# Attention in steps of three key blocks instead of two, with six tiles of exponentials and two of totals

## Chip, cores, metric

One core of one Trainium2 chip. The metric is device time in microseconds (us), the lower the better. Every run told of here is of state fast.

## The reference, cut to what matters

Hash attention on 4 batches of 8 heads, 768 tokens of 64 dimensions, then a feed-forward layer with a squared relu on 3072 tokens. All in float32; the two weight matrices come as float64 and the kernel rounds them itself.

```python
q_bits = (einsum('bhsd,dk->bhsk', q, proj) > 0);  k_bits = ...      # 6 bits a token
mask   = q_bucket[:, :, :, None] == k_bucket[:, :, None, :]
scores = where(mask, scale * q @ k.T, -1e9)
attn   = exp(scores - max); attn = attn / (sum(attn) + 1e-9)
x      = (attn @ v).transpose(0, 2, 1, 3).reshape(3072, 512)
out    = square(maximum(x @ w_in, 0)) @ w_out
```

## The kernel before

Sixteen pairs of heads go through attention one after the other. For each of the six key blocks of a pair, `score` makes scores in PSUM on PE (tile `st`; hash bits first, then features) and exponentials from them on ACT (tile `e`, one of a ring of four); `add_up` sums exponentials on DVE; `attend` multiplies them by the values on PE (tile `xo`). `finish` belongs to the pair before: hash of the next pair, totals, the last two value blocks, and the spread of the reciprocals (L445). Beside this, each pair rounds two pieces (a and b) of the float64 weights: load into `raw` on the SyncE queue, `part_weight` (L141, L145) on DVE, `place_power` (L158, L159) on ACT, `round_weight` (L169 to L177) on DVE, and a store. In six pairs DVE also makes sums for the feed-forward part. All queues run in the order written here:

```python
for pr in range(NP):                       # 16 pairs of heads
    a, b = 2 * pr, 2 * pr + 1
    ...
    if pr + 2 < NP:
        load_pair(pr + 2)                  # 8 loads of q and k, SyncE queue
    ...
    features(pr + 1, ...)                  # DVE, wanted by the next hash
    round_weight(b - 2); load_weight(b)    # load_weight: raw piece, SyncE queue
    score(pr, 0); score(pr, 1)
    finish(pr - 1, prepare)                # hash, totals, attend(pr-1, 4..5), spread
    add_up(pr, 1)
    weigh(pr + 1); normalize(pr - 1)
    part_weight(a)
    score(pr, 2); score(pr, 3)
    place_power(a)
    attend(pr, 0); attend(pr, 1)
    add_up(pr, 2); add_up(pr, 3)
    load_values(pr + 1)
    round_weight(a)
    part_weight(b)                         # here in the kernel before
    load_weight(a + 2)
    score(pr, 4); score(pr, 5)
    place_power(b)
    attend(pr, 2); attend(pr, 3)
    add_up(pr, 4)
    if pr in sums: ...                     # pairs 4, 5, 8, 9 (sums_in), 10, 11 (sums_x)
```

(Conditions for the first and last pair are cut.)

## Time and profile before

| | kernel before |
|---|---|
| median, at the time of the prediction | 908.31 us (3 runs, 908.2 to 908.92) |
| span of the profiled run, mean granted clock | 906.5 us, 0.998 |
| attention, to the first feed-forward matmul | 347 us, PE busy throughout from 35 us on |
| one pair, from spread to spread | 20.55 us |

The last line is read from the starts of the L445 matmuls (the spread, one a pair). "Pair n takes" means below: from the spread of pair n-1 to the spread of pair n, a stretch that holds all of DVE's sums of pair n. The lines of the profile that matter are in the prediction; idle time and DMA are read there as the page gives them.

### The profile page before, as it was taken

The page shows a single profiled execution, that of the slowest core. Times are in us where ns is not written, and L with a number is a line of the kernel's source. Part 1 is how long each engine was busy: PE and PEld are TensorE (multiplying, and loading weights), DVE is VectorE, ACT ScalarE, POOL GpSimd, SP SyncE. Part 2 cuts the span into 40 slices and gives each one's busy share as a digit, 9 for nine tenths or more (in the row PEclk, how much of TensorE's full clock was granted, in tenths as well). Part 3 has the DMA queues.
Part 4 walks back from the last instruction along what each step waited for, and adds up shares of the span by engine and source line. Part 5 has one row for each costly group of instructions (what it writes and reads, how often), then busy time and mean ns, then how long its engine had stood idle before and what let it go on. Part 6 is the DMA issues. An engine that isn't in the chain of part 4 may idle for free.

```text
span 906.5 us, 11859 instructions
## 1 busy us (share of the span) xinstructions
PE 882.5 (97%) x4358; PEld 504.4 (56%) x4358; DVE 697.4 (77%) x1010; ACT 364.2 (40%) x593; POOL 91.7 (10%) x149
## 2 busy tenths in 40 slices
PE   6999999999999999999999999999999999999996
PEld 3344444444444444444588864445888644458885
DVE  3788899889998885887768766667887766678775
ACT  4888787788878752222111112222111122221110
POOL 2000000000000000562100021111000211110002
PEclk9999999999999999999999999999999999999999
DMA  9467978789977425997974745546856554445566
GB/s 183 86 124 137 231 171 186 141 276 241 230 181 153 128 91 172 278 282 214 319 227 147 187 81 150 150 138 190 298 162 173 96 148 137 135 142 158 153 167 112
DMA packets 253343, 158.14 MB, mean 174 GB/s; under 512 B 166432, under 2 KB 215584, under 8 KB 253280
## 3 DMA queue, kind: packets, MB, share of 16 engines
q1 hardware_dynamic: 219984, 84.43, 40.6%
q10 hardware_dynamic: 22560, 37.50, 14.1%
q0 software_dynamic: 10736, 35.40, 13.0%
q8 instruction: 36, 0.59, 0.3%
q14 instruction: 27, 0.22, 0.1%
HBM read 119.28 MB, written 38.01 MB: 174 GB/s over the span
## 4 chain that ended last, share of the span: by engine, by line
PE 90%; DMA 4%; DVE 2%; ACT 1%; issue 1%; POOL 0%; ACTq 0%; SPq 0%; DVEq 0%
PE acc L657 54%; PE st L375 18%; PE xo L402 14%; DMA w_unit<-w_in 3%; PE tot L420 3%; PE hash L327 1%; ACT bits L337 1%; DMA out_dram<-ot 1%; DVE peaks L698 0%; DMA q_nat<-in_q_dram 0%; PE tp L300 0%; POOL out_dram L818 0%; DVE b L747 0%; ACTq L787 0%; DVE ot L811 0%
## 5 line engine op out<-in xcount | busy, mean ns | idle before, releaser
L379 ACT ACTIVATE e<-st 128x1024 f32<-128x1024 f32 x192 | 145.4, 810 | 68.8 <-PE st L375 63.9
L657 PE MATMUL acc<-x,w_unit 128*128 128x512 f32 x384 | 169.6, 593 | 0.6 <-DMA w_unit<-w_in 0.6
L375 PE MATMUL st<-feat,feat 64*128 64x512 f32 (+1 forms) x768 | 152.4, 488 | 0.0
L657 PE MATMUL acc<-b,leaf 128*128 128x256 f32 x600 | 133.3, 379 | 2.3 <-DMA leaf<-w_out 2.3
L402 PE MATMUL xo<-e,v_nat 128*64 128x512 f32 (+1 forms) x768 | 134.8, 492 | 0.0
L657 PE MATMUL acc<-t_x,w_unit 128*128 128x512 f32 x288 | 127.8, 593 | 0.2 <-ACT one L664 0.2
L657 PEld LDWEIGHTS acc<-b,leaf 128*128 128x128 f32 x600 | 113.8, 190 | 19.8 <-DMA leaf<-w_out 3.5
L657 PEld LDWEIGHTS acc<-x,w_unit 128*128 128x128 f32 x384 | 72.8, 190 | 91.5 <-issue 89.2
L402 PEld LDWEIGHTS xo<-e,v_nat 128*64 128x64 f32 x768 | 51.4, 136 | 82.4 <-issue 70.9
L657 PEld LDWEIGHTS acc<-t_x,w_unit 128*128 128x128 f32 x288 | 54.5, 190 | 70.0 <-issue 67.7
L375 PEld LDWEIGHTS st<-feat,feat 64*128 64x128 f32 x768 | 67.0, 190 | 35.5 <-issue 27.6
L392 DVE TENSOR_TENSOR total<-total,e 128x1536 f32<-128x1536 f32 x48 | 84.2, 1755 | 1.7
L746 DVE TENSOR_TENSOR h<-acc,two 128x512 f32<-128x512 f32 x24 | 16.6, 691 | 84.9 <-PE acc L657 84.9
L657 PE MATMUL acc<-t,leaf 128*128 128x256 f32 x336 | 76.8, 380 | 0.6 <-DVE t L481 0.3
L664 ACT COPY two<-acc 128x512 f32<-128x512 f32 (+1 forms) x45 | 21.9, 487 | 131.7 <-PE acc L657 128.6
L337 ACT ACTIVATE bits<-hash,lifts 32x384 bf16<-32x384 f32 x124 | 71.1, 573 | 6.5 <-PE hash L327 3.2
L664 ACT COPY one<-acc 128x512 f32<-128x512 f32 (+1 forms) x45 | 21.9, 487 | 118.8 <-PE acc L657 77.7
L657 PEld LDWEIGHTS acc<-t,leaf 128*128 128x128 f32 x336 | 63.5, 190 | 10.6 <-DVE t L481 1.1
L375 PE MATMUL st<-bits,bits 64*128 64x256 bf16 (+1 forms) x384 | 63.9, 328 | 3.4 <-ACT bits L337 2.2
L747 DVE SCALAR_TENSOR_TENSOR b<-h 128x512 f32<-128x512 f32 x96 | 64.3, 690 | 2.5
L657 PE MATMUL acc<-b_t,leaf 128*128 128x256 f32 x240 | 54.2, 380 | 1.3 <-issue 1.3
L657 PEld LDWEIGHTS acc<-b_t,leaf 128*128 128x128 f32 x240 | 45.4, 190 | 8.1 <-issue 2.1
(122 smaller groups left out, 866.4 us busy)
## 6 DMA issues: line engine op xcount, KB each, us to landing
leaf<-w_out ACTq DMA_DIRECT2D x142, 256.0 KB, 3.0
w_unit<-w_in SPq DMA_DIRECT2D x24, 896.0 KB, 5.7
raw<-in_moe_w_in_dram SPq DMA_DIRECT2D x16, 512.0 KB, 5.5
raw<-in_moe_w_out_dram SPq DMA_DIRECT2D x16, 512.0 KB, 4.5
w_out<-sums POOLq DMA_DIRECT2D x16, 448.0 KB, 8.0
v_nat<-in_v_dram SPq DMA_DIRECT2D x16, 384.0 KB, 4.7
x_all<-x_t SPq DMA_DIRECT2D x16, 384.0 KB, 3.1
x<-x_all POOLq DMA_DIRECT2D x3, 2048.0 KB, 12.5
```

What stands on the lines that cost most here:

```text
L327: nc.tensor.matmul(out=banks[g * NR_B:(g + 1) * NR_B, h, 0:HS], lhsT=projs[rows], rhs=feat[pr, w][rows, c * HS:(c + 1) * HS], start=True, ...
L337: nc.scalar.activation(out=t[h * D:h * D + NR_B, c * HS:(c + 1) * HS], in_=hashed[pr, w][at, h, 0:HS], func=ACTF.Sign, scale=HUGE, bias=li ...
L375: nc.tensor.matmul(out=st[:, h, 0:hi - lo], lhsT=src[pr, 1][rows, key], rhs=src[pr, 0][rows, lo:hi], start=first, stop=not first,)
L379: nc.scalar.activation(out=e[:, :, lo:hi], in_=st[:, :, 0:hi - lo], func=ACTF.Exp, scale=scale)
L392: nc.vector.tensor_tensor(out=totals[pr], in0=in0, in1=weights[pr, kt][:, :, 0:S], op=ALU.add)
L402: nc.tensor.matmul(out=xo[h * D:(h + 1) * D, lo:hi], lhsT=nat[pr, "v_nat"][:, h, kt * D:(kt + 1) * D], rhs=weights[pr, kt][:, h, lo:hi], s ...
L420: nc.tensor.matmul(out=tot[g * 32:(g + 1) * 32, 0:HS], lhsT=ones, rhs=src[:, h, c * HS:(c + 1) * HS], start=src is totals[pr], stop=src is ...
L657: nc.tensor.matmul(out=acc[to], lhsT=a(i), rhs=b(i), start=first and i == 0, stop=last and i == n - 1, skip_group_check=True,)
L664: nc.scalar.copy(out=t, in_=acc[of])
L746: nc.vector.tensor_tensor(out=h, in0=one, in1=two, op=ALU.add)
L747: nc.vector.scalar_tensor_tensor(out=out[:, r], in0=h, scalar=0.0, in1=h, op0=ALU.max, op1=ALU.mult)
```

## The change

Fewer, longer runs of score and value blocks: three by three instead of two by two. That needs the exponentials of a whole pair to stand, so six tiles instead of four, and a second tile of totals, as the next pair's first adds now come before the last pair's totals are used. To make room, `x_t` and the input sums fall from two buffers to one. On the way, the splitting and powers of piece b move up beside those of piece a.

```diff
-    p_x = first.enter_context(tc.tile_pool(name="p_x", bufs=2))
+    p_x = first.enter_context(tc.tile_pool(name="p_x", bufs=1))
-    NRING = 4
+    NRING = SB
-            totals[pr] = p_n.tile([P, 2, S], FP32, name="total")
+            totals[pr] = p_n.tile([P, 2, S], FP32, name="total", bufs=2)
-        sums = [p_t.tile([P, nf, NS], FP32, name=f"s_in{n}", bufs=2) for n in range(4)]
+        sums = [p_t.tile([P, nf, NS], FP32, name=f"s_in{n}") for n in range(4)]
-        for kt in (SB - 2, SB - 1):            # in finish
+        for kt in range(SB // 2, SB):
             attend(pr, kt)
 ...
-            score(pr, 0)
-            score(pr, 1)
+            for kt in range(3):
+                score(pr, kt)
+            for kt in (1, 2):
+                add_up(pr, kt)
             if pr > 0:
                 finish(pr - 1, prepare if more else None)
-            add_up(pr, 1)
 ...
             part_weight(a)
-            score(pr, 2)
-            score(pr, 3)
+            part_weight(b)
+            for kt in range(3, SB):
+                score(pr, kt)
             place_power(a)
-            attend(pr, 0)
-            attend(pr, 1)
-            for kt in (2, 3):
+            place_power(b)
+            for kt in range(3):
+                attend(pr, kt)
+            for kt in (3, 4):
                 add_up(pr, kt)
 ...
             round_weight(a)
-            part_weight(b)
             if more:
                 load_weight(a + 2)
-            score(pr, 4)
-            score(pr, 5)
-            place_power(b)
-            attend(pr, 2)
-            attend(pr, 3)
-            add_up(pr, 4)
```

## The prediction

> **What bounds the kernel now.** I first read the first part of the page, then the busy time by stretches, because an average over two stages hides each stage. The stretches are my choice: the first pair of heads (4.80 to 35.17), the other pairs (35.17 to 346.98) and the feed-forward part.
>
> ```profile
> PE 882.5 (97%) x4358; PEld 504.4 (56%) x4358; DVE 697.4 (77%) x1010; ACT 364.2 (40%) x593; POOL 91.7 (10%) x149
> ...
> 4.80:35.17 30.37, 25.17 (x149) 11.84 (x150) 16.43 (x23) 19.52 (x30) 2.21 (x11) 1.00 1.10 177
> 35.17:346.98 311.81, 311.81 (x2363) 142.46 (x2361) 269.25 (x366) 239.33 (x352) 0.79 (x1) 1.00 0.71 167
> ```
>
> The columns of a stretch are its length, then busy us of PE, weight loads, DVE, ACT, POOL, the clock and the DMA. From 35.17 on PE is busy for all 311.81 us, with DVE at 86% and ACT at 77%. So no wait is there to remove: only less time on PE itself can shorten this stage. The first pair is the exception: 5.2 us of its 30.37 are idle on PE.
>
> Next the chain that ended last, over one pair. It is nothing but PE:
>
> ```profile
> 123.02 2.74 PE xo L402 x16
> 125.76 0.08 PE xo L445 x4
> 125.84 3.34 PE st L375 x24
> 129.18 2.74 PE xo L402 x16
> 131.92 3.34 PE st L375 x24
> 135.26 2.74 PE xo L402 x16
> 138.00 3.34 PE st L375 x24
> 141.34 0.81 PE hash L327 x16
> 142.15 1.43 PE tot L420 x16
> ```
>
> A pair takes 143.58 - 123.02 = 20.56 us: three runs of two score blocks (st), three of two value blocks (xo), one hash, one total and one spread of reciprocals (L445). Last I read PE's timeline where st hands over to xo, taking starts, as ends of matmuls are modelled:
>
> ```profile
> 126.97 0.60 PE L375 MATMUL st<-feat,feat 64*128 64x256 f32 x4
> 127.40 0.38 PE L375 MATMUL st<-bits,bits 64*128 64x512 bf16 x2
> ...
> 128.59 0.60 PE L375 MATMUL st<-feat,feat 64*128 64x256 f32 x4
> 129.11 2.81 PE L402 MATMUL xo<-e,v_nat 128*64 128x512 f32 x16
> ```
>
> The same four matmuls are followed after 0.43 us by another st, but after 0.52 us by an xo. Note the forms: st has weights of 64*128 (two row tiles), xo of 128*64 (two column tiles). The hand-over costs time although nothing is waited for.
>
> **What the Trainium skill says.** (1) "TensorEngine Tiling (Array Packing)", Key Properties: a change of tiling mode, not merely of tile, drains the TensorE. The trace agrees: about 0.1 us more at the change from 64*128 to 128*64. (2) "TensorE: Matmul & The Clock Gate", Part 2, step 5 (NX overlap): in a stream the drain of one matmul overlaps the fill of the next; a drain is what a mode change loses. The page has no cost for the change, so I take it from the trace. (3) "Perfetto Trace Analysis", Tensor Engine Instruction: the end of a matmul is an estimate; here consecutive records overlap (0.60 long at 126.97, the next at 127.40), hence starts only. (4) The TensorE page's section on the array (engine queue depths): ScalarE and VectorE are strict FIFO. So program order on DVE and ACT decides what a late operand holds up; the trace shows DVE idle before L426 with later adds queued behind it.
>
> **The change, part by part.**
>
> *Fewer mode changes.* Before, a pair alternates st,st | xo,xo three times; after, st x3 | xo x3 twice. All matmuls stay. From single starts in the trace: one st block to the next inside a run is 1.617 us, so a run of two (3.34) holds 3.34 - 3.234 = 0.106 us of change; one xo block to the next is 1.291 us, so a run of two (2.74) holds 2.74 - 2.582 = 0.158 us. One round trip costs 0.264 us. Each pair loses one: runs become 3 x 1.617 + 0.106 = 4.96 and 3 x 1.291 + 0.158 = 4.03, and the pair 20.56 - 0.26 = 20.29. For pairs 1 to 15: 15 x 0.264 = 4.0 us off, all on the path.
>
> *The first pair.* In PE's timeline of the kernel before:
>
> ```profile
> 22.84 1.62 PE L327 MATMUL hash<-feat,projs 64*32 64x384 f32 x16 [0.60 <-ACT e L379]
> ...
> 29.32 0.39 PE L375 MATMUL st<-bits,bits 64*128 64x512 bf16 x2 [0.39 <-ACT bits L337]
> ...
> 31.78 0.29 PE L375 MATMUL st<-bits,bits 64*128 64x256 bf16 x2 [1.21 <-ACT e L379]
> ```
>
> PE loses 0.6 + 0.4 + 1.2, and about 0.75 in a hash twice its later 0.81 (its features came late from DVE). The steady run starts at 35.17 with six st, a hash and four xo done. After: st(0) to st(5) go through from 13.26, to 22.24 + 2 x 1.617 = 25.5; hash to 26.4; three xo to 30.4. ACT ends the exponentials 1.1 us after st, at 26.6; eight signs of 0.586 to 31.3; the powers of two weight pieces now come together, 2 x 1.37, to 34.0; only then the first exponential of pair 1. PE takes up pair 1 at 31.3 and, with three score buffers, stalls when the third is full (34.0) until the first exponential ends (35.0). At 31.3 it has done what the old one has at 35.17 less one xo (1.3): ahead by 2.6; less the stall of 1.0: 1.6 us gained.
>
> *DVE.* Its work stays; its order does not. Flip (the reciprocals) now queues behind two adds (1.75 each) of the next pair instead of ahead of one, and normalize follows it nearer. I set out a pair from the end of the spread, S, with start-to-start times from the timeline: normalize 0.1 to 2.1; splitting two pieces 2 x 0.67, to 3.4; adds of blocks 3 and 4, 3.53, to 6.9; rounding piece a waits for its power (ACT ends three exponentials at 6.0, then 1.4: 7.5), 1.93, to 9.4; features of the next pair 1.76, to 11.2; rounding piece b 1.97, to 13.2; adds of blocks 1 and 2 wait for exponentials to 15.1, to 16.9; flip to both 1.26, to 18.2. PE wants it at 4.96 + 4.03 + 4.96 + 0.81 + 1.43 + 4.03 less the last 0.1 of those: about 20.1. Slack 1.9. But six pairs (4, 5, 8, 9, 10, 11) also compute sums, 2.53 by DVE's timeline. Then features end at 13.7 (hash starts at 13.9: just in time), the adds end at 19.2, and both at 20.5: 0.4 late. What shows how tight these are already:
>
> ```profile
> 102.54 0.58 DVE L426 STREAM_TRANSPOSE flip<-tot 128x384 f32<-128x384 f32 x1 [3.21 <-PE tot L420]
> ...
> 123.09 0.58 DVE L426 STREAM_TRANSPOSE flip<-tot 128x384 f32<-128x384 f32 x1 [0.68 <-PE tot L420]
> ```
>
> DVE's only idle time in a pair is 3.2 us, in one with sums 0.7. New waits: 6 x 0.4 = 2.2 us (rounded down, as the last one or two run lighter operations). They don't pile up: the wait for the power absorbs a late normalize.
>
> *Buffers.* Six rings let a pair's exponentials stand until the next pair; two totals let add 1 start ahead of the old total's use. x_t and the input sums fall to one buffer. x_t is written once in 20 us and its DMA lands in 3.1; the sums likewise in 2.9. xo has one buffer: normalize ends at S + 2.1, the next xo at S + 4.96. Nothing here is on the path. At the seam, DVE's first result of the feed-forward part overlies x_t; it may wait 0.6 us for the DMA, and DVE then has 5.3 us idle in the trace before, so PE does not see it.
>
> *Feed-forward.* Untouched; it starts earlier and ends as much earlier.
>
> Sum: -4.0 - 1.6 + 2.2 = -3.4 us, so 908.3 - 3.4 = 904.9.
>
> **Rivals.** (a) *DVE takes the bound in more pairs.* For: 86% busy, and both waits of the new order (for exponential 2, for the spread) sit in one FIFO. Against: 1.9 us of slack in ten pairs. If 0.4 were lost in all fifteen, 6 us would eat the gain: about 908.7. (b) *No DVE wait at all,* if adds run a little closer than I laid them: 908.3 - 5.6 = 902.7. (c) *The start gives nothing:* ACT's two power pieces ahead of pair 1's exponentials stall PE longer than 1.0; the same six and fifteen then give 908.3 - 1.8 = 906.5. (d) *Hidden transfers.* The changed loading order could make a weight piece late. Against: in the list of PE's waits attention shows no DMA after the first transposes, and raw pieces land in 5.0 us with over 10 to spare. No change of time.
>
> **Range and chances.** The switch term is counted and repeated fifteen times; I trust it to 0.5 us. The start may be off by 1.5, the DVE term by 2. That gives 902.8 to 906.9. Two per cent is 18 us, more than three times anything worked out: within 2% 0.98, each side 0.01.
>
> **What would show it.** Chain: st runs of 36 in 4.96 and xo runs of 24 in 4.03, pairs of 20.29 us. PE's waits: an L445 wait on DVE of some 0.4 us in six pairs and none in others; a stall of about 1 us on ACT e near 34. DVE's waits: the idle time before flip goes, and appears before recs (L455), about 2 us in pairs without sums. If xo after xo across the longer run still costs 2.74 per two, the switch account is wrong; if L445 or hash wait in ordinary pairs, (a) holds; if pairs run at 20.29 throughout, (b).

## The result, and the profile after

911.12 us median (910.82 to 913.05, 6 runs) against 908.95 (908.2 to 910.44, 6 runs) for the kernel before: ratio 1.0027, 95% interval 1.0014 to 1.004. The prediction said 904.9, in a range of 902.8 to 906.9. It is wrong, in sign too: slower by about 2 us instead of faster by 3.4. (The two are within 2% of each other, to which it gave 0.98. Ratios here and below are the mean time of one kernel's fast runs over that of the other's of the same rounds, so not quite the ratio of the medians quoted.)

The part that the change was made for came out as worked out. The chain of the kernel after, over one pair (start, us, what):

```profile
63.39 4.96 PE st L375 x36
68.35 4.03 PE xo L402 x24
72.38 4.96 PE st L375 x36
77.34 0.81 PE hash L327 x16
78.15 1.43 PE tot L420 x16
79.57 4.03 PE xo L402 x24
```

Runs of 36 score matmuls in 4.96 us and of 24 value matmuls in 4.03, as predicted to the last digit. The pair takes 20.29.

But not every pair does. From the starts of L445 in the two traces, spread to spread:

| pair | 1 to 3 | 4 | 5 | 6 | 7 | 8 | 9 | 10 | 11 | 12 | 13 | 14 | 15 |
|---|---|---|---|---|---|---|---|---|---|---|---|---|---|
| before | 20.55 | 20.55 | 20.55 | 20.55 | 20.55 | 20.55 | 20.55 | 20.55 | 20.55 | 20.55 | 20.55 | 19.75 | 16.40 |
| after | 20.29 | 20.64 | 20.69 | 20.34 | 20.29 | 20.64 | 26.06 | 21.08 | 20.87 | 20.34 | 20.29 | 19.49 | 14.53 |

(The sums are in pairs 4, 5 and 8 to 11. The last two are shorter as the hash and then the next pair's scores fall away.) Over 20.29, pairs 4 to 12 lose 8.3 us; pair 9 alone 5.8. The account closes: first spread 0.66 us earlier, fourteen pairs 0.26 shorter (3.6), the last one 1.87 shorter, 8.3 lost: 2.1 us later at the first feed-forward matmul, which is where the traces put it (342.09 and 344.24 us after the first matmul of each).

What pair 9 loses it for is in DVE's timeline of the kernel after (start, us, what; in brackets the idle time before, and what ended it):

```profile
208.64 0.42 DVE L141 TENSOR_SCALAR power<-raw 128x512 uint32<-128x512 uint32 x1
208.97 0.42 DVE L145 TENSOR_SCALAR top<-raw 128x512 uint32<-128x512 uint32 x1
214.06 0.43 DVE L141 TENSOR_SCALAR power<-raw 128x512 uint32<-128x512 uint32 x1 [4.67 <-DMA raw<-in_moe_w_out_dram]
```

Piece a is split; piece b isn't there yet, and DVE stands for 4.67 us with the adds, the rounding and the features of the next pair queued behind. Piece b was late because of the SyncE queue, in the kernel after:

```profile
198.88 6.60 SPq L278 DMA_DIRECT2D q_nat<-in_q_dram  x4
205.52 2.23 SPq L278 DMA_DIRECT2D k_nat<-in_k_dram  x4
207.85 1.74 SPq L188 DMA_DIRECT2D w_out<-out_piece  x1
209.64 0.43 SPq L128 DMA_DIRECT2D raw<-in_moe_w_out_dram  x1
```

Issuing eight loads of q and k holds the queue for 8.8 us (ahead of them stood the four stores of pair 8's sums, 2.52 us, much as in the kernel before, 2.73), the store of the piece just rounded follows, and only then is raw issued, 3.3 us after the spread of pair 8 at 206.33; it lands 4.4 us later. ("Perfetto Trace Analysis", DMA Instruction: HWDGE, in the Trainium skill: the time shown for a DMA on this queue is the sequencer's, for lock, descriptors and semaphore, and only at its end is it free for the next instruction. This trace agrees.) The kernel before issued it at the same place in the pair (3.3 us after the spread, at 207.80), but asked for it later:

```profile
211.12 0.43 SPq L128 DMA_DIRECT2D raw<-in_moe_w_out_dram  x1
```

```profile
216.58 0.42 DVE L141 TENSOR_SCALAR power<-raw 128x512 uint32<-128x512 uint32 x1
```

The first line is from its SyncE queue, the second from its DVE: 5.5 us from issue to use, about 1 us more than a landing of 4.4. The old order was safe by one microsecond, and the change took away 5.7 (from 8.8 to some 3.1 us after the spread).

What DVE's stop did to PE, in PE's timeline of the kernel after:

```profile
219.98 0.60 PE L375 MATMUL st<-feat,feat 64*128 64x256 f32 x4
223.85 2.01 PE L327 MATMUL hash<-feat,projs 64*32 64x384 f32 x16 [3.27 <-DVE feat L314]
225.79 1.51 PE L420 MATMUL tot<-total,ones 128*32 128x384 f32 x8
```

The hash waits 3.27 us for features. And then hash and totals, 2.23 us elsewhere, take 4.62: the busy time by stretches says most of why (length, busy us of each engine, and the clock as third number from the end):

```profile
224.94:228.35 3.41, 3.41 (x24) 0.59 (x16) 3.27 (x5) 2.38 (x5) 0.00 (x0) 0.50 1.16 301
```

For 3.41 us the granted clock was a half, which can cost no more than half of that, 1.7 us. Most of the other 0.7 us of the 2.4 went before the clock fell at 224.94: the hash had begun at 223.85, but DVE ended the second half of its features only at 224.56:

```profile
223.63 0.93 DVE L314 STREAM_TRANSPOSE feat<-k_nat 128x768 f32<-128x768 f32 x1
```

So 3.3 us of waiting, 0.7 us mostly of a hash held up and 1.7 us of half clock (the last two are estimates) make up what pair 9 loses.

### The profile page after: what moved, and what is told of

Its sections match the earlier page's. It is cut to its first block, busy times and chain, and to the rows that moved or that the text cites. A ratio compares the mean times of both kernels' runs of the same rounds, so it can differ in the third digit from the quotient of the medians.

```text
span 911.1 us, 11908 instructions
## 1 busy us (share of the span) xinstructions
PE 880.5 (97%) x4358; PEld 509.3 (56%) x4358; DVE 700.6 (77%) x1012; ACT 364.1 (40%) x593; POOL 91.4 (10%) x149
## 4 chain that ended last, share of the span: by engine, by line
PE 77%; DVE 11%; DMA 7%; ACT 2%; issue 2%; POOL 0%; SPq 0%; DVEq 0%; ACTq 0%
PE acc L651 54%; PE st L375 12%; PE xo L402 8%; DMA w_unit<-w_in 3%; DVE total L392 3%; PE tot L420 2%; DMA raw<-in_moe_w_out_dram 2%; DVE feat L314 1%; PE hash L327 1%; ACT bits L337 1%; DMA out_dram<-ot 1%; DVE power L169 1%; DVE top L174 1%; ACT e L379 1%; ACT small L158 0%
## 5 line engine op out<-in xcount | busy, mean ns | idle before, releaser
L402 PE MATMUL xo<-e,v_nat 128*64 128x512 f32 (+1 forms) x768 | 131.2, 490 | 0.0
```

What stands on the lines that cost most here:

```text
L402: nc.tensor.matmul(out=xo[h * D:(h + 1) * D, lo:hi], lhsT=nat[pr, "v_nat"][:, h, kt * D:(kt + 1) * D], rhs=weights[pr, kt][:, h, lo:hi], s ...
```

## The experiments

Theory 1: the second raw piece is asked for before it has landed; DVE's queue stops, PE lacks features and its clock falls. Rival A: DVE simply has too much work in the pairs with sums. Rival B: the single buffers hold up the queue. The first four ran on one chip beside 20 runs of the kernel before (median 910.09).

### early_raw: load piece b ahead of q and k

```diff
+            if pr > 0:
+                load_weight(b)
             if pr + 2 < NP:
                 load_pair(pr + 2)
 ...
                 round_weight(b - 2)
-                load_weight(b)
```

> The changed kernel with one load moved: the raw piece b of a pair is issued on the SyncE queue ahead of the next pair's eight q and k loads instead of behind them. Theory 1 (the second raw piece lands late, now that its splitting on DVE was moved up before the adds; DVE's queue stops, PE idles for lack of features and its clock falls): DVE's waits for raw (4.7, 1.2 and 0.8 us in the changed kernel) go to zero, no hash waits over 1 us, the granted clock stays at full speed from 30 us on, and pair 9, 26.06 us from spread to spread, falls to 20.7; pairs 10 and 11 to 20.7. About 6.2 us less than the changed kernel: ratio to before 0.996, some 905. Rival A (DVE simply has too much work in the pairs with sums): pairs 8 to 11 stay above 21 us, ratio 1.002 to 1.003. Rival B (the single buffers of x_t and of the input sums hold up the SyncE queue): no change either, 1.002 to 1.003.

Measured: 906.29 us median (903.49 to 907.34, 5 runs), ratio 0.9949 (0.993 to 0.9968). Its SyncE queue:

```profile
197.11 0.84 SPq L128 DMA_DIRECT2D raw<-in_moe_w_out_dram  x1
198.01 6.87 SPq L278 DMA_DIRECT2D q_nat<-in_q_dram  x4
```

Raw now goes first, and DVE waits for raw nowhere. Pairs 8 to 11 take 20.66, 20.70, 20.44 and 20.56 us, no hash waits, and in attention the clock stays full. Theory 1 holds; rivals A and B, which had expected no change, fall as explanations of the 6.3 us. What is left, 2.06 us over pairs 4 to 12, is the prediction's own DVE term.

### late_part: split piece b after the adds again

```diff
             part_weight(a)
-            part_weight(b)
 ...
             place_power(a)
-            place_power(b)
 ...
             for kt in (3, 4):
                 add_up(pr, kt)
+            part_weight(b)
+            place_power(b)
```

> The changed kernel with one part of the change undone: the splitting of piece b on DVE, and its powers on ACT, come after the adds of blocks 3 and 4 again, 3.5 us later than in the changed kernel; the loads are untouched. Theory 1: the wait for raw in pair 9 shrinks from 4.7 to about 1.2 us and those of pairs 10 and 11 vanish; the hash waits about 0 to 0.5 us, so the clock does not fall; pair 9 from 26.06 to about 21.5; 5 us less than the changed kernel, ratio to before about 0.9975, some 906.5. Rival A (too much DVE work): the work is the same, so nothing changes, 1.002 to 1.003. Rival B (single buffers): nothing changes.

Measured: 907.11 us median (905.36 to 908.41, 6 runs), ratio 0.9962 (0.9949 to 0.9974). Pairs 9 to 11: 21.09, 20.44, 20.56 us, one wait for raw left, of 0.7 us. The same gain from the other side: supply earlier or demand later. A little better than expected.

### half_sums: spread the sums over twice as many pairs

`sums_in` makes two of its four operations in one pair and the other two, with the four stores, in the next; `sums_x` one operation a pair:

```diff
-    sums = {c // 2 * (NIN // 2) + c % 2 + NIN // 2: (sums_in, c) for c in range(4)}
-    for n in range(2):
-        sums[X_0 + 1 + n] = lambda n: sums_x(0, n), n
+    sums = {NIN // 2 + n: (sums_in, divmod(n, 2)) for n in range(8)}
+    for n in range(4):
+        sums[X_0 + 3 + n] = lambda n: sums_x(0, n // 2, n % 2), n
```

> The changed kernel with the four operations of each input sum spread over two pairs (pairs 4 to 11, two each) and the four of the x sums over pairs 12 to 15, one each; the loads are untouched. The same DVE work in all, but no pair has more than 1.4 us of it instead of 2.5. Theory 1 and the DVE term of the prediction: the 0.35 to 0.4 us by which the spread waits for its reciprocals in pairs 4, 5 and 8 vanish; raw waits of 1 to 3.5 us remain in pairs 9 and 11, where the sums' writes still stand before the loads, and cost 1 to 3 us; ratio 0.996 to 0.998, some 905 to 907. Rival A (only the amount of DVE work in one pair matters): all excess goes, pairs at 20.3 throughout, ratio 0.9935, some 903. Rival B: no change but the 2 us of the sums, 1.000.

Measured: 913.0 us median (911.53 to 914.97, 6 runs), ratio 1.0027 (1.0014 to 1.0039): a miss for all three. Pairs 4 to 7 take 20.29 as theory 1 had it, but 8, 9 and 10 take 22.94, 22.13 and 24.63. DVE of this kernel:

```profile
193.33 0.43 DVE L141 TENSOR_SCALAR power<-raw 128x512 uint32<-128x512 uint32 x1 [4.08 <-DMA raw<-in_moe_w_out_dram]
```

The stores of sums now stood in pair 7's queue, for 7.62 us ahead of q and k, and made pair 8's piece late, which had been in time. With less DVE work in each pair the waits for raw grew from 6.6 us to 13.2. So the amount of DVE work was not the cause, and what I had wrong in the expectation was to count the wait pair by pair and not to ask where the stores would go.

### two_xt: two buffers of x_t again

```diff
-    p_x = first.enter_context(tc.tile_pool(name="p_x", bufs=1))
+    p_x = first.enter_context(tc.tile_pool(name="p_x", bufs=2))
```

> The changed kernel with two buffers for x_t again (the change had cut them to one); there is room for it. Rival B (a single x_t holds up normalize or the SyncE queue): pairs 8 to 11 get faster, ratio down to 0.998 or less. Theory 1 and rival A: nothing changes, 1.002 to 1.004, pair 9 at 26 us with a hash wait of 3.3 us.

Measured: 912.22 us median (910.37 to 915.98, 12 runs), ratio 1.0036 (1.0023 to 1.0048). Pairs 9 and 10 take 24.36 and 22.90, two waits for raw of 7.1 us in all: the same loss, divided otherwise. x_t was not it. (One detail of the expectation failed: pair 9 was to take 26 us.) I did not double the single buffer of the input sums, for want of room as I saw it; no run here shows that. But early_raw kept it and lost nothing by it that shows, and before_split_up below has two of each and loses nearly the same in pairs 9 and 10.

### early_half: both, the early load and the spread sums

The diffs of early_raw and half_sums together; run on one chip beside 27 runs of the kernel before (median 909.94), as were the next two.

> The changed kernel with both: the raw piece b loaded ahead of the next pair's q and k, and the sums spread over twice as many pairs. Theory 1 with the DVE term: every pair from 1 on takes 20.30 us, no wait of DVE for raw and none of the spread for the reciprocals; the 8.3 us that the changed kernel loses in pairs 4, 5 and 8 to 11 are all back: ratio to before 0.9935, some 903, about the 902.7 that the prediction named for no DVE wait. Rival A: the same, so this run alone does not tell them apart. Rival B: 0.998 or above. If it is not below 0.996, something else than these two costs time.

Measured: 904.98 us median (902.39 to 905.55, 6 runs), ratio 0.9946 (0.9928 to 0.9964): faster than both kernels, by half a per cent. Pairs 1 to 13 take 20.29 us, DVE waits for no DMA and the spread for no reciprocals; attention ends 5.7 us earlier than before, close to the 5.6 of the prediction's rival (b). The total gains 5.0 (3.3 to 6.6 by the interval). It cannot be told from early_raw by the total time (0.9946 and 0.9949), only by the pairs.

### before_early: the control

The early load in the kernel before.

> Control: the kernel before with the raw piece b loaded ahead of q and k. In the kernel before, DVE never waits for a raw piece, so theory 1 expects no difference: ratio 0.999 to 1.001, pairs at 20.55 us. If it is faster by more than 0.2%, the load order costs time by itself and the changed kernel is not its cause.

Measured: 908.95 us median (907.28 to 910.84, 20 runs), ratio 0.9992 (0.9984 to 0.9999), pairs 1 to 13 at 20.55. The load order by itself is worth next to nothing (0.1 to 1.5 us by the interval); it matters once the splitting is early.

### before_single: more changes of tiling mode

```diff
             score(pr, 2)
+            if pr > 0:
+                attend(pr, 0)
             score(pr, 3)
 ...
-            attend(pr, 0)
+            if pr == 0:
+                attend(pr, 0)
             attend(pr, 1)
 ...
             score(pr, 4)
+            if pr > 0:
+                attend(pr, 2)
             score(pr, 5)
 ...
-            attend(pr, 2)
+            if pr == 0:
+                attend(pr, 2)
             attend(pr, 3)
```

> The kernel before with the suspected cost doubled: in the second and third run of a pair the score and value blocks alternate one by one (st, xo, st, xo) instead of two by two, so two more round trips of tiling mode in each pair from pair 1 on, with the same matmuls. If a round trip costs 0.264 us whatever the length of the run, a pair takes 20.55 + 0.53 = 21.08 us and the kernel 908.9 + 15 x 0.53 = 916.9, ratio 1.0087. If the cost lies in the score blocks (waits for exponentials hidden in the matmul records) rather than in the change of tiling, it will not scale so: value block 0 then also has more time, and the ratio stays below 1.004, or rises well above 1.012 where the exponentials of the block just scored aren't ready.

Measured: 931.92 us median (929.66 to 932.56, 4 runs), ratio 1.0249 (1.0228 to 1.0269): a miss. A pair takes 21.98, 1.43 more. In PE's timeline:

```profile
64.30 0.60 PE L375 MATMUL st<-feat,feat 64*128 64x256 f32 x4
65.75 1.51 PE L402 MATMUL xo<-e,v_nat 128*64 128x512 f32 x8 [0.85 <-PE st L375]
```

The wait is put down to PE itself, but DVE's x_t of the pair before ends at 65.64: value block 0, moved up, waits for normalize to free the only accumulator. From the start of the last st to the start of xo are 1.45 us here and 0.52 at the hand-overs where nothing is waited for: 0.9 us, which have nothing to do with the mode changes and fall in every pair. (The next expectation puts this at 0.82; the starts give 0.9, and 1.43 less the 0.53 of two round trips is 0.9 too.) I had confounded two things.

### before_single3: the cleaner form

Only the second half of that diff (st 4, xo 2, st 5, xo 3). Run on one chip with before_split_up, beside 7 runs of the kernel before (median 909.31).

> A cleaner form of the doubled cost: only the third run of a pair is broken up (st 4, xo 2, st 5, xo 3), so value block 0, which waited 0.82 us for the normalization to free its accumulator in the last trial, keeps its old place. One round trip more in each pair: 20.55 + 0.264 = 20.82 us from spread to spread, with no wait of xo; 15 x 0.264 = 4 us more, ratio 1.0044. If a round trip costs what the last trial seemed to give at first sight (1.43 us for two, 0.71 each), 21.27 us and 1.012.

Measured: 914.46 us median (914.04 to 915.34, 4 runs), ratio 1.0059 (1.0042 to 1.0076). Every ordinary pair takes 20.81 us, PE waits for nothing, and the chain shows runs of one:

```profile
70.17 1.73 PE st L375 x12
71.90 1.44 PE xo L402 x8
73.34 1.72 PE st L375 x12
75.06 1.45 PE xo L402 x8
```

1.73 + 1.44 against 1.617 + 1.291 within runs: 0.26 us for a round trip. The same cost for runs of one, two and three: a round trip between st and xo has a fixed price, whatever the length of the runs. That the price is that of the tiling mode, and not of something else in which st and xo differ, is the prediction's reading; no run here separates the two.

### before_split_up: the moved splitting alone

```diff
             part_weight(a)
+            part_weight(b)
             score(pr, 2)
             score(pr, 3)
 ...
             place_power(a)
+            place_power(b)
 ...
             round_weight(a)
-            part_weight(b)
 ...
             score(pr, 5)
-            place_power(b)
```

> One part of the change alone, in the kernel before: the splitting of piece b on DVE and its powers on ACT move up to those of piece a; the blocks still go two by two, and the buffers are as before. Theory 1: the raw piece of pair 9 lands at about 215.5 us, DVE now wants it at about 210.5, so DVE waits for raw some 5 us in pair 9 and 1 us in 8 to 11 otherwise; DVE had 0.7 us to spare in these pairs, so the hash of pair 9 waits 3 us or more for features, the clock may fall, and the kernel loses 5 to 8 us: ratio 1.005 to 1.009. If the loss belongs to the steps of three (the adds' and the reciprocals' new places on DVE) rather than to the moved splitting, this kernel keeps 20.55 us in all pairs and the ratio is 0.999 to 1.001.

Measured: 919.85 us median (916.66 to 923.16, 4 runs), ratio 1.0114 (1.0079 to 1.0149): more than expected. The profiled run shows pair 9 at 26.41 us and pair 10 at 21.78, nearly those of the changed kernel, with the same wait on DVE:

```profile
218.56 0.43 DVE L141 TENSOR_SCALAR power<-raw 128x512 uint32<-128x512 uint32 x1 [4.36 <-DMA raw<-in_moe_w_out_dram]
```

Pair 5 loses 1.07 and the first spread comes 2.1 us later, which I had not expected. At the start the powers of both pieces now stand ahead of exponentials on ACT, and PE waits for those for 2.48 us instead of 1.21; then the clock is a half from 33.24 to 36.65:

```profile
32.04 0.28 PE L375 MATMUL st<-bits,bits 64*128 64x256 bf16 x2 [2.48 <-ACT e L379]
```

So the loss belongs to the move of the splitting and its powers, and not to the steps of three or to the single buffers: put on the old kernel it costs 10 us, 8.3 in pairs 5 to 11 and 2.1 at the start, as there is no gain beside it.

## Why the prediction was wrong

*Mode changes, -4.0 us: right.* Runs, pairs and the cost of a round trip came out as given (20.29 against 20.55), and before_single3 confirms the cost with 20.81. That a drain is behind it stays the reading of the page.

*The first pair, -1.6: right.* The first spread is 0.66 us earlier with one score block more done (1.62). But 0.7 of that is luck, an estimate from the clock: it reached full speed 4.73 us after the first score matmul in the profiled run before and 3.35 us in the one after, and 1.4 us at half speed are worth 0.7. That leaves some 1.6. Profiles in which the clock was full before the first score matmul say the same: from its start to the first spread took 27.80 us in before_single, whose first pair is the old one, and 27.83 in early_raw, which has one score block more done by then. The stall of PE on the first exponentials of pair 1 was 0.89 us, for 1.0 in the prediction.

*DVE in pairs with sums, +2.2: right.* In early_raw, where it stands alone, it is 2.06.

*The failed step* is the wait that the prediction left out: in its list of DVE's operations "splitting two pieces 2 x 0.67, to 3.4" waits for nothing, and the one place that asks, rival (d), "Hidden transfers", says: "raw pieces land in 5.0 us with over 10 to spare. No change of time." It measured 6.3 us (8.3 less 2.06). The landing time was about right, 4.4 to 4.7 for the three pieces that DVE waited for. The spare time was not worked out: I took it from the order of the program, where the load stands near the top of a pair's turn of the loop and the old splitting near its end, and didn't look at when the queue issued it. In the trace before, the SyncE line at 211.12 and the DVE line at 216.58 were there to read: 5.5 us, one to spare. The change pulled the demand up by 5.7 us and left the supply. I had asked of the other waits on DVE what the new order did to them, but not of this one, because in the kernel before it did not wait at all.

*A term not in the sum* is the clock. A wait of 3.27 us on PE was followed by 3.41 us at half clock, up to 1.7 us more. "TensorE: Matmul & The Clock Gate" in the Trainium skill, Part 1, says that after an idle window of about 3.4 us the clock is halved, and such a window is 3.413 us; the length of the slow stretch agrees with the trace, that a whole window has to be idle does not (see the end).

*The rivals.* (a) did not come: no ordinary pair waited. Nor did (c), as the start shows. (b) came in early_half, where 5.7 us were gained in attention.

## What to carry to other kernels

Before an operation is moved up in a strict queue, look up in the trace of the kernel before when each of its inputs was issued and landed, and not only that nobody waited for it: an input that is in time by 1 us looks exactly like one that is in time by 10. Moved work and its loads belong together; here one line, the load ahead of eight others, turned 2 us lost into 4 to 5 gained. And where the bound engine alternates between two shapes of tile, the change-over has a price that can be read from starts, and longer runs are worth it only as long as they bring no wait.

## What the Trainium skill lacked or had wrong

- "TensorEngine Tiling (Array Packing)", Key Properties, says that a change of mode drains the engine, without a price. Here a round trip between 64*128 and 128*64 tiles cost 0.26 us, for runs of one, two and three blocks alike (20.81, 20.55 and 20.29 us a pair). No run here shows that the drain is what costs it.
- "TensorE: Matmul & The Clock Gate", Part 1, ties the fall of the clock to an idle window of about 3.4 us. Here less was enough, by this working. In each trace the changes of the clock lie a whole number of stretches of 3.413 us apart (61 in the changed kernel, from 16.73 to 224.94). Count PE's idle time in these stretches while the clock is full: the clock fell at the end of every one with 1.85 us idle or more (2.32 in the changed kernel, 2.02 in half_sums, 2.22 and 1.85 in before_split_up), and at the end of none with 1.80 or less, in all eleven traces. So where a wait lies counts, too: the 2.7 us before a hash in two_xt were divided between two stretches, with 1.03 and 1.70 us idle, and nothing fell. (An inference from PE's records, whose ends are modelled.)
- The same page calls the start of full speed run-variable. Its size here: from 1.8 us before to 5.9 us after the first score matmul in the eleven traces, and with it the first six score blocks of the new order took from 9.54 us (two_xt) to 12.39 us (half_sums), from the first matmul's start to the last one's. Runs of one kernel differ by as much (4.0 us over the 27 runs of the kernel before); that this is the cause no run shows.
- "DMA: Bandwidth & Descriptors", Issuing engines are not separate DMA queues, calls the time on the sequencer to start a DMA "usually small relative to the DMA itself". Here each of the eight loads of q and k in a pair (96 KB, landing in a median of 5.0 and 3.8 us) took the sequencer 0.3 to 5.0 us, and all eight held the SyncE queue for 5.1 us (a pair of two_xt) to 10.3 us (6.87 + 3.38 in early_raw) and once 13.5 us (early_half); everything behind them waited.
